# A fused attention and gated MLP kernel: one row group of the second chunk transposed by a DMA transfer in place of TensorE

## The chip, the cores and the metric

The kernel runs on one core of a Trainium2 chip. The metric is the device time of one execution in microseconds (us); the kernel before has a median of 711.62 us over three runs (711.37 to 711.65). The engines are TensorE (PE in the profile, its weight loads PEld), VectorE (DVE), ScalarE (ACT), GpSimd (POOL) and SyncE (SP). Transfers are issued by SyncE, ScalarE and GpSimd and carried by 16 DMA engines; in the profile q1 is the queue of SyncE, q10 that of ScalarE, q0 that of GpSimd.

## What is computed

x has 2048 rows of 1024 bf16 values. The reference, cut to what matters:

```python
xn = _layernorm(x)
s = _A_ref(xn, wqkv, wo)            # dilated sliding-window attention, 32 heads, 8 positions, step 2
g = _silu(_B_ref(xn, w1, w3, w2))   # (silu(xn @ w1) * (xn @ w3)) @ w2, inner width 3584
return x + s * g
```

## The kernel before, in words

The rows are cut into four chunks of 512, and each chunk into four row groups of 128 (`NST = 4`). Two chunks form a block. Within a block the products with a weight matrix are made by a scheme with seven products in place of eight, in the manner of Strassen and Winograd: the two chunks are the two block rows of x, the two halves of the 1024 inner dimension its block columns. Besides the transposed x of both chunks (`xT`, with the half 0 for the first chunk and 1 for the second) it needs sums of them, `xs`. The first of these, `xs0`, subtracts the first chunk's lower half from the second chunk's, over all 512 columns at once, so that it reads all four row groups of the second chunk.

The program is recorded as a list of operations by a planner (`Plan`). TensorE's operations keep the order in which they are recorded. For the other engines the planner plays the program through with costs and due times and issues each operation where it comes up there; `plan.rows` fixes the order of those near the start by name. So a change in the recorded order can move copies on ScalarE and issues on SyncE. On each engine the instructions then run strictly in order.

The change lies in the first 50 us, on chunks 0 and 1:

- `qkv_first("q", ...)` makes the first part of q for chunk 0, with the row groups of chunk 0 being transposed between the matmuls (`rows0`). Its four accumulators are copied to SBUF twice by ScalarE: a snapshot halfway (`fsnap`, into `h_sb`) and the end (`fc11`, into `qo`).
- `qkv_first("k", ...)` does the same for k, in matmul parts `kpart(j, h)` of two 512-wide matmuls each for output j and half h of the inner dimension. Between them it calls `mid(0)` to `mid(3)`, each of which transposes one row group of chunk 1. All of it has `ln_tp`: eight matmuls of 128 columns with the identity matrix as the moving operand into two PSUM banks (line 585), and two evictions by ScalarE into `xT` (line 592). The banks of the first of these transposes are the ones that the first `fc11` copies set free.
- `xn_sums` makes xs0, xs1, xs2 and xs3 on VectorE (line 442), and `qkv_sums` the sums of the weights. `plan.rows` puts VectorE's order as "... ts1_3 qs0 qs1 xs0 qs3 xs1", where `ts1_j` normalises row group j of chunk 1 in place (line 520).
- `qkv_pairs(..., first=True)` goes on with pairs of outputs: eight matmuls with xs0 (`qe`), eight with xT of chunk 1 on the same accumulators (`add3`), eight with xs1 (`up2`), eight with xs2, then eight with xs0 for the next pair, and eight with xs3 (`tail`) into the accumulators that VectorE has emptied by `qc22` and `qc12`. Between `qe` and `add3` ScalarE copies the accumulators away (`qs5`); `qfork` puts the snapshot of `fsnap` into fresh accumulators ahead of `up2`.

A transposing transfer is in the kernel already: `ln_td` issues one from ScalarE's queue, from SBUF to SBUF, for a row group of 128 x 1024 values (256 KB, runs of 256 bytes). Before the change it is used for chunks 2 and 3 alone, around 263 to 303 us:

```python
    def ln_td(c, st, xt):
        half = c % 2
        plan.op(ACT, f"td{c}_{st}", lambda: nc.scalar.dma_start_transpose(
            out=xT[:, half, :, st * P:(st + 1) * P], in_=xrow(xt, st)),
            [(xt, st)], xt_cells(half, 0, st) + xt_cells(half, 1, st) + ["turned"], 1.3, 0.0, nbytes=256 * 1024, run=256)
```

In the first 35 us SyncE issues the loads in this order: x and the first halves of the q and k weights in pieces, the second half of k's weights (1 MB, `wqkv1_1`, which the last 16 matmuls of `qkv_first("k", ...)` read), and then ten loads of 512 KB of w2. Transfers of SyncE and ScalarE take turns on eight completion semaphores; a transfer is issued when the one eight places ahead of it has landed.

At the end, `wo(3, wots, True)` multiplies the attention's result with wo, and `finish` multiplies with the gate, adds x and stores, in pieces.

Of the kernel before, what the change touches and what calls it, by code (L numbers as in the profile page):

```python
# [14 lines left out]
PE, DVE, ACT, POOL, SP = range(5)  # L15
# [291 lines left out]
def kernel(  # L307
# [12 lines left out]
    P = 128  # L320
# [4 lines left out]
    CH = 512  # L325
    BL = 1024
    NB = S // BL
    NST = CH // P
# [117 lines left out]
    def cp(name, o, a, rd, wr, occ=0.48):  # L446
        plan.op(ACT, name, lambda: nc.scalar.copy(out=o(), in_=a()), rd, wr, occ, 0.11)  # L447
# [36 lines left out]
    def f32(s):  # L484
        return s.ap()
# [198 lines left out]
    def first_at(nm, j):  # L684

        fl = j + 4 * (nm == "k")
        return lambda: h_sb[:, fl, :].bitcast(FP32), h_cells([fl], 0) + h_cells([fl], 1)

    def qkv_first(nm, wts, mid=None, rows=None):

        pa = [bank(f"f{nm}{j}") for j in range(4)]
        def part(st, ks=range(KH)):
            for j in range(4):
                mm(pa[j], [qkv_w(wts[0], k, j) for k in ks], [bx[0, 0][k] for k in ks], st == 0 and ks[0] == 0,
                   wk_cells(wts[0], ks) + xt_cells(0, 0, st), st=(st, 1))

        def kpart(j, h):
            ks = range(2 * h, 2 * h + 2)
            mm(pa[j], [qkv_w(wts[0], k, j) for k in ks], [bx[0, 0][k] for k in ks], not h,
               wk_cells(wts[0], ks) + [("xT", 0, k, st) for k in ks for st in range(NST)])  # L700

        if rows:
            rows(part)
        else:
            mid(0)
            kpart(0, 0)
            kpart(1, 0)
            mid(1)
            kpart(2, 0)
            kpart(3, 0)  # L710
            mid(2)
        for j in range(4):
            if mid is not None and j == 3:
                mid(3)
            if not rows:
                kpart(j, 1)
            dst, wr = first_at(nm, j)
            cp("fsnap", dst, pa[j].ap, [pa[j]], wr)
        for j in range(4):
            mm(pa[j], [qkv_w(wts[1], k, j) for k in range(KH)], bx[0, 1], False, wk_cells(wts[1]) + xt_cells(0, 1))  # L720
            dst, wr = home(0, nm)(j)
            cp("fc11", dst, pa[j].ap, [pa[j]], wr)
# [21 lines left out]
    def qkv_pairs(b, nm, wts, S, load=None, first=False):  # L744
        c0, c1 = 2 * b, 2 * b + 1
        I = range(2)
        sw = lambda q, j: [lambda k=k: s_half(S, q).rearrange("p (k c j) -> p k j c", k=KH, j=4)[:, k, j, :] for k in range(KH)]
        sc = lambda q: [s_at(S, q)]
        wl = lambda kh, j: [qkv_w(wts[kh], k, j) for k in range(KH)]
        for j0 in (0, 2):  # L750
            js = [j0, j0 + 1]
            pa = two("mm", f"qa{nm}{j0}") if not first else []
            for i in I if not first else ():
                mm(pa[i], wl(0, js[i]), bx[0, 0], True, wk_cells(wts[0]) + xt_cells(0, 0))
            pe = two("mm", f"qe{nm}{j0}")
            for i in I:
                mm(pe[i], sw(0, js[i]), tx[0], True, sc(0) + xs_cells(0), mark=[("qe", nm, js[i])])
            flush()
            if load is not None and j0 == 0:
                load()  # L760
            pb, sp5, su2 = two("mm", f"qb{nm}{j0}"), two("k2", "qs5"), two("k2", "qu2")
            for i in I:
                src, rd = first_at(nm, js[i]) if first else (pa[i].ap, [pa[i]])
                cp("qfork", pb[i].ap, src, rd + [("qe", nm, js[i])], [pb[i]], 0.54 if first else 0.48)
            for i in I:
                cp("qs5", lambda i=i, s=sp5: f32(s[i]), pe[i].ap, [pe[i]], [sp5[i]])
            for i in I if not first else ():
                mm(pa[i], wl(1, js[i]), bx[0, 1], False, wk_cells(wts[1]) + xt_cells(0, 1))
                dst, wr = home(c0, nm)(js[i])
                cp("qc11", dst, pa[i].ap, [pa[i]], wr)  # L770
            def up2():
                for i in I:
                    mm(pb[i], sw(1, js[i]), tx[1], False, sc(1) + xs_cells(1))
                    cp("qu2", lambda i=i, s=su2: f32(s[i]), pb[i].ap, [pb[i]], [su2[i]])

            def add3():
                for i in I:
                    mm(pe[i], sw(3, js[i]), bx[1, 1], False, sc(3) + xt_cells(1, 1))

            for part in (add3, up2) if first else (up2, add3):  # L780
                part()
            dst, wr = home2(c1, nm, j0)
            tt("qc12", add, dst, rows2(pe), rows2(su2), pe + su2, wr, BL, False)
            for i in I:
                mm(pb[i], sw(2, js[i]), tx[2], False, sc(2) + xs_cells(2))
            if b:
                dst, wr = home2(c1, nm, j0 + 4)
                tt("qc22", add, dst, rows2(pb), rows2(sp5), pb + sp5, wr, BL, False)
            else:
                for i in I:  # L790
                    dst, wr = home(c1, nm)(js[i] + 4)
                    tt("qc22", add, dst, pb[i].ap, lambda i=i, s=sp5: f32(s[i]), [pb[i], sp5[i]], wr, 512, False)

            def tail(js=js, pb=pb, j0=j0):
                for i in I:
                    mm(pb[i], wl(1, js[i] + 4), tx[3], False, wk_cells(wts[1]) + xs_cells(3))
                    dst, wr = home(c0, nm)(js[i] + 4)
                    cp("qc21", dst, pb[i].ap, [pb[i]], wr)
                if j0:
                    for c in (c0, c1):  # L800
                        if (nm, c) in park:
                            put(c, nm)

            pend.append(tail)
# [563 lines left out]
    def wo(c, wots, last=False):  # L1368
# [102 lines left out]
        if last:  # L1471
# [27 lines left out]
                tt("x_o", add, o, o, lambda: half(xrow(xt, 1), h), [xt] + cc, cc, 256, True, 4.0)  # L1499
                dma((SP, ACT)[h], "out", lambda: out_flat[rows, h * 256:(h + 1) * 256], o, cc, [], 64, 512)  # L1500

            def direct21(i, late):
                mm(pb[i], ow(1, i + 2), wt(3), False, owc(1, i + 2) + wo_tc(3))
                o, (gv, gc) = xo(0, i + 2), gate(c, 0, i + 2)
                tt("s_g", mul, o, pb[i].ap, gv, [pb[i]] + gc, xc(0, i + 2), 512, False, late)
                tt("x_o", add, o, o, lambda: xrow(xt, i + 2)[:, :CH], [xt] + xc(0, i + 2), xc(0, i + 2), 512, True, late)
                g0 = (c * NST + i + 2) * P
                dma(SP, "out", lambda: out_flat[g0:g0 + P, :CH], o, xc(0, i + 2), [], 128, 1024, late)


            p1(0)
            p5(0)
# [11 lines left out]
            finish(1, 0, 1, 0.5, slice(0, 4, 2))  # L1524
            u2(1)
            c12(1)
            finish(1, 1, 1, 1)
            c22(1)
            finish(1, 3, 1, 1.5)
            flush()  # L1530
            c21(0)
            finish(0, 2, 1, 2)
# [81 lines left out]
    for b in range(NB):  # L1614
        c0, c1 = 2 * b, 2 * b + 1
        wq = qkv_load(0, 2 if b == 0 else 1)
        if b == 0:
            plan.shift = -2.0
            for st in range(NST):
                x_load(1, st, x1)  # L1620
            plan.shift = -1.0
            for st in range(NST):
                ln_dve(1, st, x1)
            plan.shift = 0.0
            wk = qkv_load(1, 2)
            qkv_first("q", wq, rows=rows0)
            qkv_first("k", wk, lambda j: ln_tp(1, j, x1, (ACT, ACT)))
            xn_sums()
            xn_sums2()
            sq = qkv_sums(wq, 30.0)  # L1630
            for i in range(FH // 2):
                w2_load(i)
                w2_sums(i)
            qkv_pairs(b, "q", wq, sq, first=True)
        else:
            attention(c0 - 1)
            xn_sums(hold=True)
            sq = qkv_sums(wq)
            wk = []

            def second():
                xn_sum4()
                xn_sums2()
                wk.extend(qkv_load(1))

            qkv_pairs(b, "q", wq, sq, second)
        sk = qkv_sums(wk)
        wv = []
        if b:
            halo("k")  # L1650
        qkv_pairs(b, "k", wk, sk, lambda: wv.extend(qkv_load(2)), first=b == 0)
        sv = qkv_sums(wv)

        w1o = []

        def first(b=b):
            if b:
                w1o.extend(wo_load())
            else:
                up_load(b, 0)  # L1660

        qkv_pairs(b, "v", wv, sv, first)
        if b == 0:
            w_sums(0)
        else:
            wo(c0 - 1, w1o)
        for fb in range(FB):
            up_step(b, fb)
        attention(c0)
        mlp_down(b)  # L1670
        wots = wo_load()
        if b:
            wo_back()
        else:
            wo_sums(wots)
        wo(c0, wots)
# [33 lines left out]
```

## Time and profile before

| What | Value |
|---|---|
| Median of 3 runs | 711.62 us |
| Profiled execution, its own time | 711.47 us |
| Its span, first to last instruction | 709.7 us |
| DMA traffic over the span | 162.13 MB, mean 228 GB/s |
| DMA share of the first 18 us (first of 40 slices) | 90% or more |
| ScalarE's DMA queue | 8592 packets, 2.16 MB, 1.9% of 16 engines |

How to read the rows that follow. A timeline row has the start in us, the duration, the engine, the line of the kernel, the operation, out<-in with the program's names, sizes, and the count of instructions merged; "q" behind an engine's name is its sequencer, which issues transfers. Matmuls are pipelined, so that a row's duration reaches a little into the next row; the distance between starts is the better measure. A DMA row by queue has packets, MB, and the time that the packets took as a share of 16 engines over the window asked for. An issue row has size and the median time from issue to landing.

### The profile page before, as it was taken

Reading aid. Unit: us, or ns where it says so; the run is one execution under the profiler, and the core shown is the slowest. Engines: PE = TensorE matmul, PEld = TensorE weight load, DVE = VectorE, ACT = ScalarE, POOL = GpSimd, SP = SyncE. Lnnn points to the kernel's source line nnn. Section 1 sums busy time; section 2 is a strip of 40 time slices with the busy share of each in tenths; the row PEclk is TensorE's granted clock in tenths of the full one; section 3 lists DMA queues with packets and bytes.
Section 4 is the critical chain, followed back from the end, with each engine's and each line's share of the span. In section 5 each row is a group of like instructions: output and inputs, shape, how many; then the busy total and the mean of one; then the engine's idle time right before and its main releaser. Section 6 shows DMA issues by size and latency. Waiting matters only on the chain.

```text
span 709.7 us, 9970 instructions
## 1 busy us (share of the span) xinstructions
PE 702.5 (99%) x3634; PEld 368.7 (52%) x3634; DVE 687.2 (97%) x959; ACT 412.0 (58%) x763; POOL 38.6 (5%) x78
## 2 busy tenths in 40 slices
PE   8999999999999999999999999999999999999997
PEld 5655555555555544744555555555555554455443
DVE  7997999999999999999999999998999999999987
ACT  7754566668766798622635355668665654431333
POOL 0010111001200000000100000000000000010000
PEclk9999999999999999999999999999999999999999
DMA  9889877568865669895824559979655644547633
GB/s 325 328 320 322 292 294 245 200 202 274 255 210 180 245 214 216 223 276 180 334 79 169 178 194 348 327 255 300 210 173 202 212 168 157 186 135 235 231 141 103
DMA packets 132209, 162.13 MB, mean 228 GB/s; under 512 B 13248, under 2 KB 109120, under 8 KB 126656
## 3 DMA queue, kind: packets, MB, share of 16 engines
q1 hardware_dynamic: 117744, 127.35, 55.6%
q0 software_dynamic: 5824, 31.99, 11.6%
q10 hardware_dynamic: 8592, 2.16, 1.9%
q8 instruction: 28, 0.46, 0.3%
q14 instruction: 21, 0.17, 0.1%
HBM read 112.72 MB, written 38.27 MB: 213 GB/s over the span
## 4 chain that ended last, share of the span: by engine, by line
PE 98%; DVE 1%; DMA 1%; SPq 0%; issue 0%; DVEq 0%
PE mm L433 88%; PE mm L1020 6%; PE mm L1284 3%; DVE r L442 1%; DMA r<-in_A_x_dram 1%; PE mm L585 1%; PE mm L1479 0%; SPq L456 0%; DVE small L512 0%; DVE r L520 0%; PE mm L572 0%; DVEq L1705 0%; DVE small L519 0%; DVEq L442 0%
## 5 line engine op out<-in xcount | busy, mean ns | idle before, releaser
L433 PEld LDWEIGHTS <-r 128*128 128x128 bf16 (+1 forms) x2064 | 217.8, 108 | 194.1 <-issue 0.5
L433 PE MATMUL mm<-xs,r 128*128 128x512 f16 x1056 | 251.4, 379 | 0.0
L433 PE MATMUL mm<-xT,r 128*128 128x512 bf16 (+1 forms) x1008 | 232.3, 370 | 0.0
L447 ACT COPY k<-mm 128x512 f32<-128x512 f32 (+1 forms) x256 | 133.2, 534 | 58.1 <-PE mm L433 47.4
L433 PE MATMUL mm<-r,h_sb 128*128 128x512 bf16 (+1 forms) x704 | 154.1, 379 | 0.0
L433 PEld LDWEIGHTS <-h_sb 128*128 128x128 f16 (+1 forms) x800 | 78.1, 98 | 93.7 <-DVE h_sb L442 0.5
L442 DVE TENSOR_TENSOR att<-att 128x1024 bf16<-128x1024 bf16 (+6 forms) x176 | 104.4, 608 | 3.9 <-ACT att L877 2.8
L447 ACT COPY mm<-mm 128x512 f32<-128x512 f32 (+1 forms) x121 | 62.1, 517 | 52.7 <-PE mm L433 40.8
L442 DVE TENSOR_TENSOR att<-qo,kT 128x2048 bf16<-128x2048 bf16 x64 | 77.8, 1222 | 3.6 <-ACT kT L447 2.9
L450 ACT ACTIVATE k<-k 128x512 bf16<-128x512 f32 x56 | 33.4, 625 | 64.7 <-DVE k L442 64.7
L442 DVE TENSOR_TENSOR att<-E,vT 128x2048 bf16<-128x2048 bf16 x56 | 66.8, 1220 | 0.0
L442 DVE TENSOR_TENSOR r<-r,r 128x256 f16<-128x256 f16 (+7 forms) x99 | 63.7, 658 | 1.4 <-PE mm L433 1.1
L442 DVE TENSOR_TENSOR h_sb<-mm,k 128x1024 bf16<-128x1024 f32 (+1 forms) x56 | 61.1, 1106 | 0.0
L1020 PEld LDWEIGHTS <-r 128*128 128x128 f16 x392 | 38.3, 98 | 28.4
L450 ACT ACTIVATE h_sb<-mm 128x512 bf16<-128x512 f32 x60 | 35.9, 600 | 20.1 <-PE mm L433 20.0
L442 DVE TENSOR_TENSOR k<-mm,k 128x1024 f32<-128x1024 f32 (+1 forms) x44 | 44.9, 1027 | 0.8 <-PE mm L433 0.3
L1020 PE MATMUL mm<-xT,r 128*128 128x256 f16 x224 | 42.8, 273 | 0.0
L447 ACT CAST k<-mm 128x512 bf16<-128x512 f32 x56 | 32.4, 585 | 15.9 <-PE mm L433 15.8
L442 DVE TENSOR_TENSOR h_sb<-h_sb 128x1024 f16<-128x1024 bf16 (+3 forms) x51 | 39.3, 802 | 0.0
L442 DVE TENSOR_TENSOR qo<-qo,att 128x2048 bf16<-128x2048 bf16 x32 | 39.1, 1223 | 0.1
L442 DVE TENSOR_TENSOR r<-r 128x1024 f16<-128x1024 bf16 (+2 forms) x64 | 36.5, 575 | 0.0
L442 DVE TENSOR_TENSOR h_sb<-h_sb,k 128x2048 bf16<-128x2048 bf16 x28 | 34.2, 1221 | 0.2 <-ACT k L447 0.2
(109 smaller groups left out, 508.9 us busy)
## 6 DMA issues: line engine op xcount, KB each, us to landing
r<-in_B_w_dram SPq DMA_DIRECT2D x42, 512.0 KB, 5.0
s_dram<-r POOLq DMA_DIRECT2D x14, 1024.0 KB, 5.8
r<-t_dram SPq DMA_DIRECT2D x16, 896.0 KB, 6.2
r<-s_dram SPq DMA_DIRECT2D x14, 1024.0 KB, 4.9
r<-in_B_w_dram SPq DMA_DIRECT2D x12, 896.0 KB, 4.9
r<-in_A_wqkv_dram SPq DMA_DIRECT2D x10, 1024.0 KB, 7.4
h_sb<-in_B_w_dram SPq DMA_DIRECT2D x14, 512.0 KB, 11.1
t_dram<-h_sb POOLq DMA_DIRECT2D x7, 1024.0 KB, 5.1
```

The lines of the kernel that those rows point to most:

```text
L433: nc.tensor.matmul(cut(ps.ap()), lhsT=lhs[k](), rhs=cut(rhs[k]()), start=(first and k == 0), stop=(last and k == n - 1), skip_group_check= ...
L442: plan.op(DVE, name, lambda: fn(out=o(), in0=a(), in1=b()), rd, wr, occ, 0.08, late=late)
L447: plan.op(ACT, name, lambda: nc.scalar.copy(out=o(), in_=a()), rd, wr, occ, 0.11)
L450: plan.op(ACT, name, lambda: nc.scalar.activation(out=o(), in_=a(), func=ACTF.Silu), rd, wr, occ, 0.11, table="silu")
L585: nc.tensor.matmul(tp.ap()[:, k * P:(k + 1) * P], lhsT=xrow(xt, st)[:, kt * P:(kt + 1) * P], rhs=ident[:], start=(k == 0), stop=(k == KH - ...
L1020: nc.tensor.matmul(ps.ap()[:, h * 256:(h + 1) * 256], lhsT=lhs[k](), rhs=rhs[k](), start=first and k == 0, stop=False, skip_group_check=True)
L1284: nc.tensor.matmul(ps.ap()[:, col * 256:(col + 1) * 256], lhsT=lhs[k](), rhs=r()[:, k, :], start=first and k == 0, stop=False, skip_group_ ...
```

## The change

Four edits. Row group 0 of chunk 1 is turned by `ln_td`, a transposing transfer on ScalarE's queue, where the other three stay with `ln_tp`. The call `mid(2)` goes behind `kpart(0, 1)`. In the first pairs (`first=True`) both `qs5` copies come ahead of both `qfork` copies, and the forks are made to wait for them. At the end the store of piece (1, 1) is left out and its rows go with those of piece (1, 3), in one store in place of two. (`direct21`, which nothing calls, is taken out.)

```diff
@@ qkv_first @@
             kpart(2, 0)
             kpart(3, 0)
-            mid(2)
         for j in range(4):
             if mid is not None and j == 3:
                 mid(3)
             if not rows:
                 kpart(j, 1)
+            if mid is not None and j == 0:
+                mid(2)
             dst, wr = first_at(nm, j)
             cp("fsnap", dst, pa[j].ap, [pa[j]], wr)
@@ qkv_pairs @@
-            for i in I:
-                src, rd = first_at(nm, js[i]) if first else (pa[i].ap, [pa[i]])
-                cp("qfork", pb[i].ap, src, rd + [("qe", nm, js[i])], [pb[i]], 0.54 if first else 0.48)
-            for i in I:
-                cp("qs5", lambda i=i, s=sp5: f32(s[i]), pe[i].ap, [pe[i]], [sp5[i]])
+            def fork():
+                for i in I:
+                    src, rd = first_at(nm, js[i]) if first else (pa[i].ap, [pa[i]])
+                    cp("qfork", pb[i].ap, src, rd + [("qe", nm, js[i])] + (sp5 if first else []), [pb[i]], 0.54 if first else 0.48)
+
+            def take5():
+                for i in I:
+                    cp("qs5", lambda i=i, s=sp5: f32(s[i]), pe[i].ap, [pe[i]], [sp5[i]])
+
+            for part in (take5, fork) if first else (fork, take5):
+                part()
@@ wo, last @@
-            finish(1, 1, 1, 1)
+            finish(1, 1, 1, 1, False)
             c22(1)
-            finish(1, 3, 1, 1.5)
+            finish(1, 3, 1, 1.5, slice(1, 4, 2))
@@ block 0 @@
-            qkv_first("k", wk, lambda j: ln_tp(1, j, x1, (ACT, ACT)))
+            qkv_first("k", wk, lambda j: ln_tp(1, j, x1) if j else ln_td(1, j, x1))
```

In the built program the transposing transfer stands on ScalarE behind the fourth `fsnap` of q and ahead of the first `fc11`. It takes its turn on the semaphores ahead of `wqkv1_1`, so that from there each later transfer of SyncE uses the semaphore after the one it had. VectorE's order is unchanged. On SyncE the two loads of the first w1 and w3 pieces go ahead of one of the later w2 loads.

More of the change, by code (lines that the diff above doesn't have):

```diff
@@ L1500, in final @@
                 dma((SP, ACT)[h], "out", lambda: out_flat[rows, h * 256:(h + 1) * 256], o, cc, [], 64, 512)
[L1502 to L1508, printed above, removed]
             p1(0)
```

## The prediction

> **What bounds the kernel now.** I began with the page: span, busy shares, the chain that ended last.
>
> ```profile
> span 709.7 us, 9970 instructions
> PE 702.5 (99%) x3634; PEld 368.7 (52%) x3634; DVE 687.2 (97%) x959; ACT 412.0 (58%) x763; POOL 38.6 (5%) x78
> PE 98%; DVE 1%; DMA 1%; SPq 0%; issue 0%; DVEq 0%
> ```
>
> TensorE is the chain. The profiled execution's own time is 711.47 us for a span of 709.7 us, and lies 0.15 us under the median of 711.62 us; the sum below goes on 711.47. Next comes the timeline of the stretch that the change touches, TensorE first.
>
> ```profile
> 17.46 0.61 PE L585 MATMUL mm<-ident,r 128*128 128x128 bf16 x8
> 17.91 1.04 PE L433 MATMUL mm<-xT,r 128*128 128x512 bf16 x4
> 20.10 0.61 PE L585 MATMUL mm<-ident,r 128*128 128x128 bf16 x8
> 21.85 0.61 PE L585 MATMUL mm<-ident,r 128*128 128x128 bf16 x8
> 26.20 1.89 PE L433 MATMUL mm<-xs,r 128*128 128x512 f16 x8
> 27.92 2.01 PE L433 MATMUL mm<-xT,r 128*128 128x512 bf16 x8
> 29.76 7.07 PE L433 MATMUL mm<-xs,r 128*128 128x512 f16 x32
> 36.67 1.89 PE L433 MATMUL mm<-xT,r 128*128 128x512 bf16 x8
> ```
>
> Each row starts before the one ahead ends: no gap. The pitch is (36.67 - 29.76) / 32 = 0.216 us for a 512-wide matmul. So time is gained only by giving TensorE less to do, and any stall put in is lost for good, since nothing later is idle to make it up. VectorE in the same stretch:
>
> ```profile
> 14.38 0.55 DVE L520 TENSOR_SCALAR r<-r,small 128x1024 bf16<-128x1024 bf16 x1
> 19.20 0.49 DVE L520 TENSOR_SCALAR r<-r,small 128x1024 bf16<-128x1024 bf16 x1
> 20.78 2.55 DVE L442 TENSOR_TENSOR r<-r,r 128x2048 f16<-128x2048 bf16 x2
> 23.25 1.22 DVE L442 TENSOR_TENSOR xs<-xT 128x2048 f16<-128x2048 bf16 x1
> 32.62 2.42 DVE L442 TENSOR_TENSOR qo<-mm,k 128x512 bf16<-128x512 f32 x3
> 26.20:36.67 10.47, 10.47 (x49) 5.68 (x48) 10.32 (x13) 6.23 (x12) 0.00 (x0) 1.00 0.66 242
> ```
>
> The last row gives the busy times by engine between 26.20 and 36.67 us: TensorE 10.47 of 10.47 us, VectorE 10.32. So VectorE has 0.15 us to spare there. The row at 23.25 is xs0, the first sum that reads every row group of the second chunk's transposed x; the three at 32.62 empty accumulators that TensorE writes again.
>
> **The change, part by part.** *Removed from TensorE:* the eight transposing matmuls of row group 0 (17.46). The next row starts 17.91 - 17.46 = 0.45 us later, so the gain is 0.45 us, if nothing waits instead. Two evictions of 0.5 us go from ScalarE.
>
> *Order of copies in the first pairs.* Both qs5 copies now come ahead of both qforks. The matmuls at 27.92 last 29.76 - 27.92 = 1.84 us against 27.92 - 26.20 = 1.72 us for the eight before them: 0.12 us of stall, the most this can win. A loss is excluded up to 0.1 us, as the forks are needed only by the matmuls at 29.76.
>
> *mid(2) moved* behind the next two matmuls. Its row group is ready at 19.20 + 0.49 = 19.69 us; its turn, 20.10, would come at 20.10 - 0.45 = 19.65 without the move and at 20.08 with it. Cost nothing; without it 0.04 us.
>
> *Store at the end.* One SyncE store fewer; its rows go with a later one.
>
> ```profile
> 704.33 2.37 DVE r L442 x8
> 706.70 0.34 DVEq L1705
> ```
>
> The chain ends on VectorE, with stores behind it. The joined store (256 KB) is issued with row 3's, some 3 us before the last. Nothing; at worst 0.1 us.
>
> *Added: the transposing transfer.* ScalarE issues it right behind the fourth fsnap:
>
> ```profile
> 15.19 0.59 ACT L447 COPY h_sb<-mm 128x512 f32<-128x512 f32 x1
> 298.72 0.58 ACT L447 COPY k<-mm 128x512 f32<-128x512 f32 x1 [0.18 <-DVE att L442]
> 298.74 1.25 ACTq L601 DMA_TRANSPOSE xT<-r  x1
> ```
>
> An issue follows closely on the start of the copy ahead, so it begins at about 15.3 us (its rows are normalised at 14.38 + 0.55 = 14.93). It holds ScalarE for 1.25 us. Queued behind it are the four copies of q; the first two free the accumulators for the next transposes, and are done by 16.6 + 0.5 + 0.6 = 17.7 us; TensorE wants the accumulators at 17.46 + 4 x 0.216 = 18.3. Covered by 0.6 us.
>
> When does it land? The kernel has eight such transfers later on:
>
> ```profile
> L601 ACTq DMA_TRANSPOSE xT<-r x8: 1247/1296/4459, 263.1 to 302.9; - x8
> DMA to landing us min/median/max: 3.3/7.2/11.8
> q10 hardware_dynamic: 8448, 2.10, 25.6%
> ```
>
> (The last row is the ScalarE queue, packets and MB, from 262 to 315 us: 8448 / 8 = 1056 packets each, 66 for each of 16 engines.) They run beside light or moderate traffic. At 15 us the queue of SyncE is packed with weights:
>
> ```profile
> h_sb<-in_B_w_dram SPq DMA_DIRECT2D x1, 512.0 KB, 12.8
> q1 hardware_dynamic: 785, 1.54, 104.6%
> ```
>
> The load issued at 14.1 us takes 12.8 us to land, and from 16 to 20 us q1 alone fills the engines: 1.046 x 16 x 4 us / 785 = 85 ns a packet. How two queues share:
>
> ```profile
> q1 hardware_dynamic: 997, 1.00, 106.6%
> q1 hardware_dynamic: 406, 0.42, 80.0%
> q10 hardware_dynamic: 411, 0.11, 30.9%
> ```
>
> The first row is all there was from 300 to 303 us, after the transfer issued at 298.74: no packet of q10 for over 4 us, while q1 worked off what was queued. Then, from 303.4 to 304.9 us, 411 packets against 406: one for one, q10's 0.309 x 16 x 1.5 us / 411 = 18 ns each. So beside 85 ns packets the transfer needs 66 x (85 + 18) = 6.8 us. Start-up I take from this row, 4.3 us, as it alone had two transfers queued ahead; the lower bound is the transfer of 291.44:
>
> ```profile
> 291.44 1.25 ACTq L601 DMA_TRANSPOSE xT<-r  x1
> q10 hardware_dynamic: 54, 0.01, 12.4%
> ```
>
> That is q10 from 293.0 to 293.5 us: first packets 1.6 to 2.1 us after issue, say 1.85. Landing follows the last packet by an estimated 0.4 us. So it lands at 15.3 + 4.3 + 6.8 + 0.4 = 26.8 us.
>
> [...]
>
> *What is late then.* VectorE works in order: xs0 waits at its head, and behind it the other sums, the weight sums and the three rows of 32.62. It starts at 26.85 instead of 23.25, 3.6 us late, and makes up 0.15. The last of the three then ends at 35.04 + 3.45 = 38.5 us. TensorE needs it for the fourth matmul group behind 29.76 (28 matmuls on: 29.76 + 28 x 0.216 = 35.80, so 0.76 us of slack before). TensorE loses 3.6 - 0.15 - 0.76 = 2.7 us. Its earlier wait at 26.20 for xs0 (26.85 + 1.25 = 28.1, or 1.9 us) is inside this, and so are the 0.45 us won before. The weights share the engines too: 1056 x 18 ns / 16 = 1.2 us, which the 1 MB load that TensorE needs by 22.3 us feels first; that stall is inside the 2.7 as well.
>
> Sum: 711.47 + 2.7 = 714.2 us.
>
> **Rivals.**
> 1. *Hidden.* The transfer lands by 23 us, 7.7 us after issue. For: the median of eight is 7.2 us. Against: 6.8 us of packets alone plus any start-up exceeds it, and none of the eight met a queue of 85 ns packets this long. Time: 711.47 - 0.45 - 0.12 = 710.9 us. [...]
> 2. *Shares from the start.* With 1.85 us of start-up it lands at 15.3 + 1.85 + 6.8 + 0.4 = 24.35; xs0 is 1.15 us late, less 0.91 of slack: 711.7 us. For: the transfer of 291.44. Against: that one met a queue about to run dry.
> 3. *Behind all that is queued.* First packets only once q1 has served what was issued before: 15.3 + 12.8 = 28.1 us, then 1.1 us in one go (first row below: 1956 packets in 2 us with no other traffic), landing at 29.3; 6.05 - 0.91 = 5.1 us lost, 716.6 us; shared one for one it is 5.7 us more. For: the four empty microseconds.
>
> ```profile
> q10 hardware_dynamic: 1956, 0.48, 116.4%
> 268.06 4.46 ACTq L601 DMA_TRANSPOSE xT<-r  x1
> ```
>
> 4. *ScalarE is held.* The issue takes 4.46 us, as at 268.06, instead of 1.25. The first two copies of q are done at 15.3 + 4.46 + 1.1 = 20.9; TensorE, wanting the second at 18.5, loses 2.4 us, less the 0.57 won: 713.3 us, unless the landing is worse. Against: there two others were in flight on the same queue; here it is empty.
>
> **How the numbers follow.** Forecast 0.45 (its own range 712.6 to 716, start-up of 3 to 6 us), hidden 0.14, shares from the start 0.19, behind all 0.14, ScalarE held 0.08. About 0.2% (1.4 us) is what a measurement can tell from no change. Faster by that much isn't in reach: all that can be won is 0.57 us, so 0.02. Slower: 0.41 of the forecast's 0.45, all 0.14 of rival 3, 0.06 of rival 4: 0.61. The rest, 0.37, is no change. The range runs from 710.8 (hidden) to 717.5, which leaves out the upper part of rival 3.
>
> **What would show it.** The transposing transfer at about 15.3 us on ScalarE's queue, landing near 26.8; an idle VectorE of 3 us or more from about 22.8 us, ended by that transfer; a TensorE gap ahead of the first xs matmuls and a second one near 37 us ahead of the fourth group behind them; later rows shifted by one constant; stores at the end as before. If VectorE's gap is missing, rival 1 or 2 holds; if the gap reaches beyond 28.5 us, rival 3; if ScalarE's copies of q move by over 2 us, rival 4. A new stall after 40 us would make the sum wrong in another place.

## The result, and the profile after

The changed kernel takes 715.43 us (median of 4 runs, 714.82 to 715.80) beside 711.50 us for the kernel before, measured with it: a ratio of 1.0051, 95% interval 1.0037 to 1.0066. It is slower by 3.9 us. In a later measurement of five runs it was slower by 4.7 us (716.34 beside 711.62), a ratio of 1.0061 (1.0048 to 1.0073). The profiled execution took 715.40 us, 3.93 us more than the one of before.

First the page of the changed kernel: span, and the shares of the chain that ended last.

```profile
span 713.6 us, 9898 instructions
PE 92%; DMA 3%; ACT 3%; DVE 1%; issue 1%; SPq 0%; DVEq 0%
```

Before, the chain was 98% TensorE and 1% transfers. Now transfers take 3% of it, and more than half of that is a single one. (The 3% of ScalarE lie almost all between 248 and 268 us; the rows on both sides of that stretch are late by the same time, so nothing is lost there.) The chain of waits between 13 and 42 us names the transfer (start, us, what):

```profile
14.60 11.44 DMA xT<-r
26.05 0.03 issue
26.07 0.05 DVEq L442
...
26.17 1.23 DVE r L442
27.39 1.15 DVE xs L442
...
28.58 12.40 PE mm L433 x49
```

The transposing transfer is issued at 14.60 and lands at 26.05. What follows it is not xs0 but a sum of weights (`r`, line 442); xs0 comes behind that. The same in the timelines, ScalarE, then VectorE, then TensorE:

```profile
14.60 1.93 ACTq L601 DMA_TRANSPOSE xT<-r  x1
14.83 0.60 ACT L447 COPY h_sb<-mm 128x512 f32<-128x512 f32 x1
16.58 1.56 ACT L447 CAST qo<-mm 128x512 bf16<-128x512 f32 x3 [1.15 <-PE mm L433]
20.18 1.22 DVE L442 TENSOR_TENSOR r<-r,r 128x2048 f16<-128x2048 bf16 x1
26.17 1.23 DVE L442 TENSOR_TENSOR r<-r,r 128x2048 f16<-128x2048 f16 x1 [4.77 <-DMA xT<-r]
27.31 1.22 DVE L442 TENSOR_TENSOR xs<-xT 128x2048 f16<-128x2048 bf16 x1
36.56 2.42 DVE L442 TENSOR_TENSOR qo<-mm,k 128x512 bf16<-128x512 f32 x3
28.58 3.55 PE L433 MATMUL mm<-xs,r 128*128 128x512 f16 x8 [3.04 <-DVE xs L442]
31.95 1.91 PE L433 MATMUL mm<-xT,r 128*128 128x512 bf16 x8
33.70 7.07 PE L433 MATMUL mm<-xs,r 128*128 128x512 f16 x32
40.60 1.89 PE L433 MATMUL mm<-xT,r 128*128 128x512 bf16 x7
```

The order of VectorE is qs0 (20.18), qs1 (26.17), xs0 (27.31). qs1 waits 4.77 us for the transfer, although it reads none of its data. On TensorE the row at 28.58 has the gap (3.04 us ahead of it), and its eight matmuls take 31.95 - 28.58 = 3.37 us where they took 1.72. The stretch before, in and behind the gap shows why (window, length, busy us of TensorE, its weight loads, VectorE, ScalarE and GpSimd, then granted clock, DMA share, GB/s):

```profile
20.00:25.40 5.40, 5.34 (x35) 3.70 (x34) 1.40 (x2) 5.40 (x11) 0.00 (x0) 1.00 1.10 389
25.40:28.50 3.10, 0.14 (x1) 0.00 (x0) 2.33 (x3) 0.59 (x1) 0.00 (x0) 1.00 1.03 370
28.50:32.00 3.50, 3.42 (x9) 1.19 (x9) 3.50 (x5) 0.59 (x1) 0.00 (x0) 0.51 1.05 386
32.00:36.00 4.00, 4.00 (x20) 2.11 (x19) 4.00 (x5) 2.56 (x5) 0.00 (x0) 1.00 0.51 187
```

Behind the gap TensorE runs at a granted clock of 0.51 for some 3.4 us. From 33.70 on every row is later than before by one constant: 33.70 - 29.76 = 3.94, 36.56 - 32.62 = 3.94, 40.60 - 36.67 = 3.93, and at the end, VectorE's last row of before and of after:

```profile
706.41 0.62 DVE L442 TENSOR_TENSOR r<-r,r 128x256 bf16<-128x256 bf16 x2
```

```profile
710.33 0.62 DVE L442 TENSOR_TENSOR r<-r,r 128x256 bf16<-128x256 bf16 x2
```

710.33 - 706.41 = 3.92 us. So the loss is made ahead of 34 us, in the gap and behind it, and nothing of it comes back.

The transfer itself, DMA packets by queue (packets, MB, share of 16 engines), first from 14.6 to 18.7 us, then from 18.7 to 25.1:

```profile
q1 hardware_dynamic: 800, 1.56, 103.5%
...
q1 hardware_dynamic: 1061, 2.05, 89.8%
q10 hardware_dynamic: 1036, 0.26, 18.9%
```

For 4.1 us after the issue no packet of q10, ScalarE's queue, and then one for one with q1: 1036 against 1061.

### The profile page after: what moved, and what is told of

It is laid out like the page before. It is cut to its first block, busy times and chain, and to the rows that moved or that the text cites. A ratio compares the mean times of both kernels' runs of the same rounds, so it can differ in the third digit from the quotient of the medians.

```text
span 713.6 us, 9898 instructions
## 1 busy us (share of the span) xinstructions
PE 701.0 (98%) x3570; PEld 368.9 (52%) x3626; DVE 687.1 (96%) x959; ACT 411.1 (58%) x761; POOL 38.6 (5%) x78
## 4 chain that ended last, share of the span: by engine, by line
PE 92%; DMA 3%; ACT 3%; DVE 1%; issue 1%; SPq 0%; DVEq 0%
PE mm L433 83%; PE mm L1027 6%; PE mm L1291 3%; DMA xT<-r 2%; DVE r L442 1%; ACT k L531 1%; ACT k L534 1%; DMA r<-in_A_x_dram 1%; DMA r<-in_B_w_dram 1%; ACT k L447 0%; PE mm L585 0%; ACT mm L447 0%; ACT L537 0%; DVE xs L442 0%; ACT r L544 0%
## 5 line engine op out<-in xcount | busy, mean ns | idle before, releaser
L433 PE MATMUL mm<-xT,r 128*128 128x512 bf16 (+1 forms) x968 | 227.3, 369 | 2.1
```

Source lines behind the costliest of these rows:

```text
L433: nc.tensor.matmul(cut(ps.ap()), lhsT=lhs[k](), rhs=cut(rhs[k]()), start=(first and k == 0), stop=(last and k == n - 1), skip_group_check= ...
```

## The experiments

Single executions of one kernel differ by a microsecond and more (no_td below: 710.83 to 713.91 us). In the traced one of 713.91 us, of a kernel without the transfer, TensorE's timeline has a wait of 1.76 us for the first weights; before and after have no such wait there:

```profile
9.14 0.71 PE L433 MATMUL mm<-xT,r 128*128 128x128 bf16 x8 [1.76 <-DMA r<-in_A_wqkv_dram]
```

So beside the medians I use a difference within one trace: the end (start plus duration of VectorE's last row) less the landing of the transfer. For the changed kernel that is 710.33 + 0.62 - 26.05 = 684.90 us. In the table the landing is the issue plus its time to landing in the trace.

| Kernel | Median, us | Before, measured with it | Ratio (95%) | Landing | End less landing |
|---|---|---|---|---|---|
| changed kernel | 715.43 | 711.50 | 1.0051 (1.0037 to 1.0066) | 26.05 | 684.90 |
| no_td | 711.29 | 711.55 | 0.9999 (0.9990 to 1.0008) | none | |
| td_alone | 716.21 | 711.55 | 1.0068 (1.0054 to 1.0082) | 28.07 | 685.16 |
| unread_x1 | 715.53 | 711.55 | 1.0051 (1.0036 to 1.0067) | 26.47 | 684.94 |
| unread_other | 711.62 | 711.55 | 1.0002 (0.9993 to 1.0012) | 26.18 | not waited for |
| xs0_first | 714.87 | 712.03 | 1.0044 (1.0030 to 1.0057) | 26.32 | 683.80 |
| warm | 715.43 | 712.03 | 1.0048 (1.0034 to 1.0062) | 26.41 | 684.10 |
| warm_xs0 | 714.49 | 712.03 | 1.0038 (1.0026 to 1.0051) | 26.24 | 683.79 |
| hold_w2 | 711.84 | 712.03 | 0.9997 (0.9988 to 1.0006) | 22.01 | not waited for |
| after_again | 716.34 | 711.62 | 1.0061 (1.0048 to 1.0073) | 26.96 | 684.84 |
| warm_again | 715.20 | 711.62 | 1.0049 (1.0036 to 1.0061) | 26.53 | 684.21 |
| hold_8 | 713.51 | 711.62 | 1.0030 (1.0018 to 1.0041) | 24.45 | 684.14 |
| hold_again | 711.79 | 711.62 | 1.0002 (0.9993 to 1.0010) | 21.75 | not waited for |

### Is it the transfer? (no_td, td_alone)

One takes the transfer out of the changed kernel, the other adds nothing but the transfer to the kernel before.

```diff
 no_td, against the changed kernel
-            qkv_first("k", wk, lambda j: ln_tp(1, j, x1) if j else ln_td(1, j, x1))
+            qkv_first("k", wk, lambda j: ln_tp(1, j, x1))
 td_alone, against the kernel before
-            qkv_first("k", wk, lambda j: ln_tp(1, j, x1, (ACT, ACT)))
+            qkv_first("k", wk, lambda j: ln_tp(1, j, x1) if j else ln_td(1, j, x1))
```

> The changed kernel with row group 0 of x1 turned by TensorE again; the other edits of the change (copies first, the third hook's place, one store at the end) stay. Theory, that the transfer alone costs the time: 711.35 to 711.65 us, VectorE's qs1 and xs0 back to back at about 23 us. Rival, that the reordered copies, the moved hook or the merged store cost something: between 712.5 and 715.4 us.

> The kernel of before with the transfer as its only edit. Theory, that the transfer alone costs the time: 715.2 to 715.7 us, with xs0 at about 27.5 us and a clock of about 0.5 for some 3.4 us behind TensorE's gap. Rival, that the other edits cost part of it: below 714.8 us.

no_td took 711.29 us, no different from before: the other three edits cost nothing that can be measured. td_alone took 716.21 us, above the 715.2 to 715.7 expected. In its profiled execution the transfer was issued at 16.71 us, 2.1 us later than in the changed kernel, after a late start. Measured from the landing it is 685.16 against 684.90 and 684.84, so the other edits win back at most about 0.3 us once the transfer is there. The transfer is the whole loss.

### Which wait: the turned rows, the buffer, or the traffic? (unread_x1, unread_other)

In both kernels TensorE turns all four row groups, and a transfer of the same size is issued at the same place into a part of vT that nothing reads before it is rewritten. The two differ in the source alone.

```diff
...
-            o.emit()
+            if extra and o.name == "fc11":
+                extra()
+                extra = None
+            o.emit()
...
+    plan.extra = lambda: nc.scalar.dma_start_transpose(out=vT[:, :, HALO:HALO + P], in_=xrow(x1, 0))
 unread_other: the source is the first q weight tile (x0w[0])
...
+    plan.extra = lambda: nc.scalar.dma_start_transpose(out=vT[:, :, HALO:HALO + P], in_=x0w[0].ap()[:, 0:D])
```

> TensorE turns all four row groups again; the same transfer, of the same source (row group 0 in x1's buffer), is issued at the same place by ScalarE into a part of vT that nothing reads before it is rewritten, so no instruction waits for its data. Theory, that qs1 waits because its output takes x1's buffer, which the transfer still reads: qs1 starts at the landing, about 26 us, xs0 behind it, and the time is 714.5 to 715.5 us. Rival, that only the wait for the turned data costs: qs1 at about 23.2 us and 711.4 to 711.9 us.

> As unread_x1, but the unread transfer takes its 128x1024 source from the first q weight tile instead of x1's buffer, so that neither its source nor its destination holds anyone up; what is left of it is its traffic and ScalarE's 1.9 us issue. Theory, that traffic and issue cost next to nothing and the waits are all: 711.4 to 711.9 us. Rival, that a share of the loss comes from weights landing later or from ScalarE being held: 712.5 us or more, with a wait of TensorE for a DMA or for ScalarE between 14 and 25 us.

unread_x1, VectorE and then TensorE:

```profile
26.60 1.23 DVE L446 TENSOR_TENSOR r<-r,r 128x2048 f16<-128x2048 f16 x1 [3.71 <-DMA vT<-r]
27.74 1.22 DVE L446 TENSOR_TENSOR xs<-xT 128x2048 f16<-128x2048 bf16 x1
29.01 2.33 PE L437 MATMUL mm<-xs,r 128*128 128x512 f16 x8 [2.13 <-DVE xs L446]
31.13 3.18 PE L437 MATMUL mm<-xT,r 128*128 128x512 bf16 x8
```

unread_other, the same sums and TensorE's first xs matmuls:

```profile
23.38 1.23 DVE L446 TENSOR_TENSOR xs<-xT 128x2048 f16<-128x2048 bf16 x1
26.26 1.89 PE L437 MATMUL mm<-xs,r 128*128 128x512 f16 x8
```

Nobody reads what unread_x1's transfer writes, and still qs1 waits 3.71 us for it, and the time is that of the changed kernel: 715.53 us, a hair above the 714.5 to 715.5 expected. qs1 writes the weights' sum into the buffer of x1, the transfer's source, and starts 0.13 us behind the landing (26.60 against 26.47). With the source elsewhere the wait is gone and the time is 711.62 us, with the same 256 KB beside the same loads, issued at 14.62 us. So traffic and issue cost nothing that can be measured, and the buffer alone is enough for the whole loss. The opposite case, in which qs1 writes elsewhere and only xs0 waits for the turned rows, was not run.

### What is between the landing and the end? (xs0_first, warm, warm_xs0, after_again, warm_again)

xs0_first puts xs0 ahead of qs1. warm gives TensorE 14 products of zeros in the gap. warm_xs0 has both, with nine products.

```diff
 xs0_first
-        "rc1_2 ba1_3 ts1_2 rc1_3 ts1_3 qs0 qs1 xs0 qs3 xs1",
+        "rc1_2 ba1_3 ts1_2 rc1_3 ts1_3 qs0 xs0 qs1 qs3 xs1",
 warm, in front of the first qe, into the accumulator that it starts anew
...
+                        for _ in range(14):
+                            nc.tensor.matmul(ps.ap(), lhsT=ident[:], rhs=zero, start=True, stop=True)
```

> The changed kernel with VectorE's order qs0, xs0, qs1, qs3, xs1 instead of qs0, qs1, xs0, qs3, xs1: xs0 starts at the landing and TensorE's qe products about 1.15 us sooner. Theory of two chains (TensorE's, and VectorE's work from the landing to the products it hands to the second accumulation, each of which alone gives almost the same end): VectorE has as much to do as before, so only some 0.7 us come back, 714.5 to 715.0 us. Rival of one chain (xs0's start is what counts): 1.15 us or more come back, 714.3 us or less.

> The changed kernel with 14 products of zeros (128x512, about 0.22 us each, written over by the product behind them) ahead of the first qe, in TensorE's gap. Theory: the granted clock stays at 1.00 after the gap, the eight qe matmuls take 0.22 us each instead of 0.43, and with two chains some 0.7 us come back: 714.5 to 715.0 us. Rival, that the lower clock costs nothing since VectorE sets the end there: 715.2 to 715.7 us. Second rival, one chain on TensorE: 1.6 us back, 713.8 us.

> Both edits together (VectorE's order with xs0 first, and 9 products of zeros in the gap, which is then shorter). Theory of two chains: no more than either alone, 714.5 to 715.0 us, as VectorE's chain from the landing stays. Rival of one chain: the gains add, 713.0 to 713.9 us.

> The changed kernel once more, beside the other three on one chip. The runs so far give, from one trace to the next, an end (VectorE's last row) 684.9 us behind the transfer's landing. Expected: 0.45 to 0.60% above the kernel before, and an end within 0.15 us of landing + 684.9.

> The changed kernel with 14 products of zeros in TensorE's gap, once more, beside the changed kernel on one chip. Theory, that the lower clock costs what VectorE's chain lets through (the first trace ended 684.1 us behind the landing, 0.8 less than the changed kernel): its median is 0.5 to 1.0 us below that of after_again. Rival, that the clock costs nothing: the two medians agree within 0.3 us.

warm on TensorE, with its last row on VectorE:

```profile
28.95 1.89 PE L433 MATMUL mm<-xs,r 128*128 128x512 f16 x8
32.40 6.21 PE L433 MATMUL mm<-xs,r 128*128 128x512 f16 x28
39.30 1.02 PE L433 MATMUL mm<-xs,r 128*128 128x512 f16 x4 [0.69 <-DVE qo L442]
709.89 0.62 DVE L442 TENSOR_TENSOR r<-r,r 128x256 bf16<-128x256 bf16 x2
```

The eight matmuls take 1.89 us again, the granted clock from 25.90 to 36.00 us is 1.00, and TensorE reaches the 32 matmuls 32.40 - 26.41 = 5.99 us behind the landing instead of 33.70 - 26.05 = 7.65, and then, 28 matmuls on, waits 0.69 us for VectorE's three rows. So there are two chains from the landing to that place, and the slower clock had hidden VectorE's behind TensorE's. The end comes 684.10 and 684.21 us behind the landing in the two traces of warm, 684.90 and 684.84 in the two of the changed kernel: the clock costs 0.6 to 0.8 us. The first median of warm, 715.43 us, fell into the window of the rival, so the two were run side by side: 716.34 - 715.20 = 1.14 us, a little above the 0.5 to 1.0 expected, and against the rival. The two intervals overlap, though, so the traces carry this more than the medians. (after_again itself came as expected from the landing, and with 0.61% a hair above its window.)

The mean granted clock of each execution, traced or not, says more. Some 3.4 us at half clock take 3.4 x 0.5 / 713.6 = 0.0024 off that mean. A mean of 1.000 therefore leaves no room for such a stretch, and 0.996 has room for more than one. Three executions of the changed kernel have 0.996 to 0.998 and took 715.40 to 715.80 us; the fourth has 1.000 and took 714.82. In after_again four have 0.996 to 0.998 (716.25 to 716.84 us), and one has 1.000 (714.47). So the clock does not fall in every execution of the same kernel, and those in which it stays up are the shortest. How much of that is their start is not known, as they were not traced.

xs0_first, VectorE and TensorE:

```profile
26.42 1.22 DVE L442 TENSOR_TENSOR xs<-xT 128x2048 f16<-128x2048 bf16 x1 [4.58 <-ACT kT L447]
27.69 1.89 PE L433 MATMUL mm<-xs,r 128*128 128x512 f16 x8 [1.89 <-DVE xs L442]
31.11 1.92 PE L433 MATMUL mm<-xT,r 128*128 128x512 bf16 x8 [1.52 <-DVE r L442]
```

xs0 starts 0.1 us behind the landing, the gap shrinks to 1.89 us, and the granted clock from 27.70 to 32.80 us is 1.00. (The profile names ScalarE's copies of kT as the releaser of xs0. But in the kernel before xs0 starts at 23.25 and those copies only at 24.35, so xs0 does not wait for them; the transfer had landed at 26.32.) But add3 at 31.11 then waits 1.52 us for a weight sum: behind xs0 the other sums moved, and qs3, which add3 multiplies with, came one place later too, at 29.83 us. So the edit moves more than was meant, and is no clean test of two chains against one. What it shows: the end is 1.1 us nearer to the landing (683.80), and warm_xs0 gains nothing over it (683.79). The two losses do not add: in these two traces the gap is short or filled, and the clock does not fall (a mean of 1.000 in both).

### Why does it land so late? (hold_w2, hold_8, hold_again)

SyncE's w2 loads are issued behind the transfer's landing: all ten of them, or, in hold_8, the last eight.

```diff
-        for o in self.simulate():
-            o.emit()
+        held = []
+        for o in self.simulate():
+            if held is not None and o.name.startswith("w2q"):
+                held.append(o)
+                continue
+            o.emit()
+            if o.name == "td1_0":
+                self.hold()
+                for h in held:
+                    h.emit()
+                held = None
...
+    plan.hold = lambda: nc.sync.dma_start(out=vT[0:1, 0, HALO:HALO + 64], in_=xT[0:1, 1, 0, 0:64])
```

> The changed kernel, but SyncE issues the ten w2 loads only after the transfer has landed (a 128-byte transfer that reads the turned rows stands ahead of them), so that the load queue runs empty at about 20 us. Theory, that the transfer is late because it shares the DMA engines one for one with the loads: it lands at 21 to 23 us, qs1 and xs0 wait for nothing that matters, TensorE has no gap, and the row group's 0.9 us of TensorE time is saved: 710.5 to 711.2 us, below the kernel before. Rival, that the transfer is slow by itself whatever the other queue does: it lands at 25 us or later, and the time is 714.5 us or more. Second rival, that the held w2 loads are late for VectorE's sums: 712 us or more with a wait for them between 36 and 45 us.

> As hold_w2, but the first two w2 loads (0.5 MB each) go out ahead of the transfer and only the other eight are held, so that the load queue has about 2.7 us more to move beside the transfer. Theory, that the landing moves with the length of the load queue and the time with the landing: it lands at 23.2 to 24.5 us, and the end comes 684.1 (clock kept) to 684.9 us (clock lowered) behind it, that is 0.3 to 2.4 us behind the kernel before. Rival, that only holding all loads helps, since the transfer is slow by itself: it lands at 25.5 us or later, and the time is that of the changed kernel.

> hold_w2 once more, beside the kernel before on one chip, for the sign of a small gain. In its first trace the stretch from the fourth row group of x0 being turned to the end was 0.58 us shorter than before. Theory: 0.3 to 0.9 us below the kernel before. Rival, that the hidden transfer gains nothing: within 0.2 us of it.

hold_w2: the transfer's time from issue to landing in the list of DMA issues, then, in the timelines, the issue, xs0 and the first xs matmuls:

```profile
xT<-r ACTq DMA_TRANSPOSE x1, 6.4
```

```profile
15.56 2.11 ACTq L610 DMA_TRANSPOSE xT<-r  x1
23.77 1.22 DVE L451 TENSOR_TENSOR xs<-xT 128x2048 f16<-128x2048 bf16 x1
26.34 1.89 PE L442 MATMUL mm<-xs,r 128*128 128x512 f16 x8
```

hold_8: VectorE's qs1, and TensorE at the two places:

```profile
24.57 1.23 DVE L453 TENSOR_TENSOR r<-r,r 128x2048 f16<-128x2048 f16 x1 [2.61 <-DMA xT<-r]
26.99 1.89 PE L444 MATMUL mm<-xs,r 128*128 128x512 f16 x8 [0.83 <-DVE xs L453]
37.33 1.02 PE L444 MATMUL mm<-xs,r 128*128 128x512 f16 x4 [0.69 <-DVE qo L453]
```

The landing goes with the length of the load queue: 11.4 us after the issue with all w2 loads beside it, 9.2 with two, 6.4 with none. The time goes with the landing. hold_8 lands 1.6 us sooner than the changed kernel and, with the clock kept (1.00 from 26.20 to 30.40 us), ends 684.14 us behind it, 713.51 us in all; in hold_w2 nothing waits for the transfer, and the loss is gone. Nor does VectorE wait for a held load: its only wait from 36 to 60 us is 0.8 us for TensorE.

Is hold_w2 then faster than before, by TensorE's saved 0.45 us? From the start of the fourth turned row group of x0 to the end it takes 694.95 us (12.10 to 707.05) and hold_again 695.00 (11.58 to 706.58), where the kernel before takes 695.53 (11.50 to 707.03). The medians, 11 runs each, show no gain: ratios 0.9997 and 1.0002, and 711.84 and 711.79 us are both against what was expected. A gain of 0.5 us (a ratio of 0.9993) lies inside the first interval and at the edge of the second, so whether it is there stays open. No version here beats the kernel before by a measured amount.

## Why the prediction was right, and where it was off

714.2 us was predicted and 715.43 measured; direction and the larger part of the mechanism held, two terms of the sum were missing, and one was too large. The errors have opposite signs and offset each other in part.

**A stall is lost for good: right.** From the start of the 32 matmuls to the end it is 677.27 us before (29.76 to 707.03), and 677.25 after (33.70 to 710.95).

**The other edits and ScalarE's hold: right.** no_td and unread_other are within measurement of before. The issue took 1.93 us, not 1.25, and the first copy of q still waited 1.15 us for TensorE and not TensorE for it; rival 4 falls.

**The landing: 26.8 predicted, 26.05 measured.** The issue came at 14.60 instead of 15.3; start-up was 4.1 us (4.3 predicted), and sharing and landing took 26.05 - 18.7 = 7.35 us (7.2 predicted). Within these, the packets took about what was predicted (18.7 to 25.4 us, 6.7 instead of 6.8) and the landing behind the last one more (0.65 us instead of the 0.4 that was put down without a row; before, the transfer of 291.44 landed 0.5 us behind its last packet). The step was right, and the earlier issue is nearly all of the difference. Half of that was read wrongly: the issue did not follow the start of the copy ahead here, but came 0.23 us before it (14.83). The other half is luck, as TensorE's fourth turned row group of x0 shows, before, in the changed kernel, and in after_again:

```profile
11.50 0.61 PE L585 MATMUL mm<-ident,r 128*128 128x128 bf16 x8
11.12 0.61 PE L585 MATMUL mm<-ident,r 128*128 128x128 bf16 x8
12.10 0.61 PE L585 MATMUL mm<-ident,r 128*128 128x128 bf16 x8
```

The traced execution of the changed kernel started 0.38 us early. From this row to the end it takes 4.30 us more than before (710.95 - 11.12 against 707.03 - 11.50), and after_again 4.17 us more.

Rival 2, sharing from the start, falls, as 18.7 less 14.60 shows; so does rival 3, since the two loads issued from 13 to 14.6 us took 11.8 us to land in the median, and the transfer's packets ran beside them. From 18.7 us on the two queues moved about as many packets (1036 against 1061 up to 25.1 us); why q10 moved none in the 4.1 us before is not shown.

**What waits for it: the step that failed.** "xs0 waits at its head" was read from the data alone. qs1 stands ahead of xs0, writes into the transfer's source and starts only behind the landing (26.17 against 26.05), so xs0 started not 0.05 but 27.31 - 26.05 = 1.26 us behind the landing. unread_x1 shows that this wait exists without any reader of the data. The wait of xs0 for the turned rows that the prediction described is real too: in xs0_first xs0 starts 0.1 us behind the landing, and the median is still 2.8 us above the kernel before.

**From xs0 to the end: right, with the clock kept.** The prediction has xs0 at 26.85 and 2.7 us lost, which is an end at 707.03 + 2.7 = 709.73, 682.88 us behind xs0. In warm xs0 starts at 27.68 and the end is 710.51, 682.83 behind it, and the second gap that was announced is there, 0.69 us. In the changed kernel it is missing, as the clock had made TensorE later than VectorE.

**The clock: not thought of.** A gap was predicted (1.9 us there), but no price for what follows it. The measured gap was longer by the missed wait (3.04 us), and the clock at 0.51 in the 3.4 us behind it cost 0.7 us (0.6 to 0.8 by the traces of warm).

The sum again: 2.7, less 0.75 for the landing, plus 1.14 for qs1 and 0.07 for its hand-over, plus 0.7 for the clock, is 3.86 us; the two profiled executions differ by 3.93. Without the early start of the traced execution the term for the landing would be about 0.4 instead of 0.75, and the loss about 4.2 us.

## What to carry to other kernels

Here, moving work from an engine to a DMA moved the release of its source buffer to the landing (26.05 us, for which qs1 waited 4.77 us): list who writes that buffer next, not only who reads the result. The transfer on the second queue landed 11.4, 9.2 or 6.4 us after the issue, with all w2 loads, two or none of them beside it, so look at what is queued at that moment before pricing such a transfer. In the traces half clock followed gaps of TensorE of 2.1 to 3.0 us, which in the changed kernel cost 0.6 to 0.8 us: where the busiest engine gets such a gap, price a slower clock behind it too.

## What the runs showed of the hardware that was not expected

The granted clock fell to half behind gaps of TensorE, at once or late. In the changed kernel it fell at once, behind 3.04 us. In unread_x1 TensorE was idle for 2.1 us (windows as above):

```profile
26.90:29.00 2.10, 0.00 (x0) 0.00 (x0) 2.10 (x3) 0.59 (x1) 0.00 (x0) 1.00 1.01 359
29.00:30.60 1.60, 1.59 (x7) 0.81 (x7) 1.60 (x2) 0.53 (x1) 0.00 (x0) 0.91 1.05 392
30.60:34.00 3.40, 3.40 (x10) 1.25 (x9) 3.40 (x4) 1.66 (x4) 0.00 (x0) 0.54 1.00 370
```

A mean of 0.91 over 1.60 us is 0.29 us at half clock, and 0.54 over 3.40 us is 3.13 us. So TensorE ran at full clock for 1.3 us behind the gap, and then for 3.4 us at half. In xs0_first, after gaps of 1.89 and 1.52 us that ended 3.4 us apart, it stayed at 1.00. So in these three traces half clock followed the gaps of 3.04 and 2.1 us, and not those of 1.89 and 1.52. That is no fixed threshold: as said above, single executions of the changed kernel have a mean clock of 1.000, so that it did not fall in them as it did in the traced one. And in no_td's trace, with its wait of 1.76 us ahead of 9.14 us, the mean is 0.997, and eight turning matmuls take 1.06 us at 12.00 where eight take 0.62 at 6.32.

The transposing transfer was not quick with little beside it either. In hold_w2, packets by queue from 18.6 to 22.0 us:

```profile
q10 hardware_dynamic: 1056, 0.26, 82.9%
q1 hardware_dynamic: 131, 0.24, 18.8%
```

With little other traffic (131 packets of q1) the 1056 packets took 0.829 x 16 x 3.4 / 1056 = 43 ns each on average, against 0.189 x 16 x 6.4 / 1036 = 19 ns beside full loads in the changed kernel, and the transfer landed 3.4 us after its first packet. Why is open.
